# A RWKV-6 attention block with a SiLU MLP on one core: where a unit's first keys and another unit's diagonal are issued

## The chip, the cores and the metric

The kernel runs on one core of one Trainium2 chip. The metric is the device time of one execution in microseconds; the median of several executions is given. The core has five engines that take their instructions in order from queues of their own and wait for one another with semaphores: TensorE (PE in the profile, with its weight loads as PEld), VectorE (DVE), ScalarE (ACT), GpSimd (POOL) and SyncE (SP), which issues most of the DMAs here.

## The reference

Two blocks follow each other. The first is a linear attention with a decay per channel, over 4 batches, 8 heads, 768 tokens and a head size of 48:

```
for t in range(S):
    cur = einsum('bhd,bhe->bhde', u * k[t], v[t])
    y[t] = einsum('bhd,bhde->bhe', r[t], state + cur)
    state = w[t] * state + einsum('bhd,bhe->bhde', k[t], v[t])
```

The output y is laid out as 3072 tokens of 384 channels (all heads side by side) and is the input x of the second block, an MLP without gate:

```
h = x @ w_in            # 384 -> 2048
out = (h * sigmoid(h)) @ w_out   # 2048 -> 384
```

Everything is float32.

## The kernel before, in words

**Units.** The work is cut into 12 units. Unit i is one chunk of 128 tokens of two batches (all 8 heads); the units take the chunks in order, and the two pairs of batches in turn. Tokens or channels lie on the partitions as each step needs it. The first unit is number 0, so "the third unit" is `unit 2` in the code and below, and "the fourth" is `unit 3`.

**The attention of a unit.** Inside a chunk the score of a query against an earlier key needs the product of all decays between them. The kernel builds it in 7 levels. At level l the chunk is cut into blocks of 2^l tokens, and the queries in each odd block meet the keys in the even block ahead of it. Between the levels the keys and the queries are multiplied by the products of the decays of their blocks, so that after the last level they carry the decay to the ends of the chunk. The steps, with the names that stand in the code:

- `turn`: raw r, k and w are turned so that channels lie on the partitions (DVE's L374, from unit 2 on). The tiles are `tr`, `tk` and `tw`. `tk` has more rows than `tr`: in further places, called X, lie the keys that a level's scores read.
- `product` (POOL L422): products of neighbouring decays for the next level.
- `odd_ones` (ACT L659) copies keys of the odd blocks of level 0 into X, and `start_keys(own=True)` (POOL L669, two multiplies) writes the first multiplied keys there. Both together fill what level 1's scores read. `start_keys(own=False)` (two more of L669) multiplies keys in their own place, and is first needed by level 1's `odd_keys` (ACT L615).
- `grow_keys` (POOL L645, two multiplies) and `grow_queries` (DVE L627) go on to the next level. `prepare` makes the queries of a level in a new tile (DVE L779, ACT L781), so that two levels' scores can be computed in one `burst`.
- scores (PE L703 or L711) go to PSUM. Levels under 5 are copied into the tile `score` under a mask (DVE L721), levels 5 and 6 by plain copies of blocks (ACT L800, eight of 32 rows and four of 64).
- The diagonal: a token's own score is r*k*u summed over the channels, and since level 0 is computed along with it, a token's score against the one ahead of it too. `bonus` multiplies (POOL L448, L450, L452), `bonus_sum` sums (DVE L457, L461) and sends the sums by four small DMAs to their partitions (L467). `bonus_spread` copies them into the tile `both_b` (ACT: one L595 and four L597) and reverses the second batch's (DVE shuffle L598). `bonus_write` puts them into `score` under a mask (DVE L604, two copies of 128 x 1024 elements). Units 4 and later do the same for blocks of 8 tokens: `block_bonus` (POOL L507), `block_sum` (DVE L541) and `block_write` (DVE L577, of the same size as L604).
- `turn_apart`, `turn_k` (PE L819, ACT L827), `y_state`, `y_values` (PE L843, L850, L864) and `update` (PE L892) make y and the new state. L850 is the first that reads `score`.

**The MLP of a unit.** `up(i, m)`, m from 0 to 7, multiplies x with a slice of w_in (PE L1000, 12 instructions) into one of two PSUM buffers `p_h`, and ACT applies SiLU (L1009). From unit 1 on the second matrix is applied as a scheme of seven products of half size, `quarter(i, 0)` to `quarter(i, 6)` (PE L1066, 16 instructions each), that write into two PSUM buffers `p_o` in turn; `sums` (DVE L1048) makes the differences that the scheme multiplies, and DVE's L1075 (for quarter 0 ACT's L1073) takes each product out of PSUM. Unit 0's second matrix is applied plainly (`down`, PE L1022).

**Rounding of the weights.** The weights w_in and w_out come in 16 pieces of 768 KB. Each goes through ACT (L223, L225: `head_weight`; L231: `tail_weight`), DVE (L242, L243: `join_weight`) and POOL (L255: `add_weight`) before it is used. Pieces 10 to 15 run while unit 1's MLP and unit 2's attention begin; `piece(10 + m)` is followed by the list `others[m]`.

**What sets the order.** The order in which the Python code calls the steps is the order in every engine's queue; there is no scheduler that changes it. The calls for units 0 to 2 are written out by hand at L1107 to L1163. From unit 3 on `mix(i)` gives lists of steps for the attention of unit i, and between two lists the loop at L1165 puts one or two steps of the MLP of units i - 2 (`downs`: the quarters) and i - 1 (`ups`: up steps, with `sums`). For unit 3 the number of MLP steps behind each list is

```
room = (1, 1, 0, 2, 1, 1, 1, 1, 1, 2, 2, 1, 1) if i < NPAIR
```

so two up steps stand behind the list with `prepare(3, 5)`, and two behind the list with `burst(3, 5)`.

Of the kernel before, what the change touches and what calls it, by code (L numbers as in the profile page):

```python
# [38 lines left out]
def kernel(  # L39
# [11 lines left out]
    nc = tc.nc  # L51
# [4 lines left out]
    NL = 7  # L56
# [875 lines left out]
    def both(fn, i, *args):  # L932
        return [(fn, i, b, *args) for b in range(NB)]

    def block_loads(i, names="wkr"):
        return [(load_blocks, i, name, g) for name in names for g in range(4)]

    def mix(i):

        ahead = i + 1 < len(units)  # L940

        def at(now, *steps):
            return steps if now else ()

        def bonus_steps(j, *steps):
            return [(block_bonus, j, x) for x in steps]

        def sum_steps(j, *steps):
            return [(block_sum, j, x) for x in steps]

        def turns(j):
            return [*both(turn, j, "w"), (product, j, 0), *both(turn, j, "k")]

        def start(j):
            return [*[(product, j, l) for l in range(1, NL)], (grow_own, j, 1)]

        end = [[*at(ahead, *bonus_steps(i + 1, 0, 1, 2, 3))],
               [*at(i < len(units) - NB, (turn_apart, i), (turn_k, i)), (y_state, i), *both(y_values, i), *at(ahead, *turns(i + 1)),
                (sums, i - 1, FH // 2 - 2), *both(update, i), *at(not ahead, (move_x, i))]]
        if i < NPAIR:  # L960
            groups = [[*both(turn, i, "w"), (product, i, 0)],
                      [*both(turn, i, "k"), (odd_ones, i)], [*both(turn, i, "r"), (start_levels, i), (prepare_keys, i, 1)],
                      [(prepare, i, 1), *[(product, i, l) for l in range(1, NL)]],
                      [(burst, i, 1), (keep_level, i, 1)],
                      [(keep_level, i, 2), (go_on, i, 2)],
                      [(prepare, i, 3), (reverse_v, i), (bonus, i, 0)],
                      [(burst, i, 3), (keep_level, i, 3), (bonus_sum, i, 0), (bonus, i, 1), (bonus, i, 2)],
                      [(keep_level, i, 4), (go_on, i, 4), (bonus_sum, i, 1), (load_rk, i + 1), (load_u,)],
                      [(prepare, i, 5), (make_block_mask,), (bonus_spread, i), (bonus_write, i)],
                      [(burst, i, 5), (keep_level, i, 5), (keep_level, i, 6), (go_on, i, 6)], *end]  # L970
        else:
            groups = [[*both(turn, i, "r"), (grow_own, i, 0)], [*start(i), *sum_steps(i, 0, 1), *bonus_steps(i, 4, 5), (move_x, i - 1)],
                      [(odd_keys, i, 2), (grow_keys, i, 2, False), (grow_queries, i, 2), *sum_steps(i, 2)],
                      [(prepare, i, 3), *bonus_steps(i, 6, 7)],
                      [(burst, i, 3), (keep_level, i, 3), *sum_steps(i, 3, 4), (block_move, i), *at(ahead, (load_rk, i + 1))],
                      [(keep_level, i, 4), (go_on, i, 4)],
                      [(prepare, i, 5), (reverse_v, i)],
                      [(block_spread, i), (block_write, i)],
                      [(burst, i, 5), (keep_level, i, 5), (keep_level, i, 6), (go_on, i, 6)], *end]

        loads = [*at(i >= NPAIR and ahead, *block_loads(i + 1, "r")), *at(i + NSLOT < len(units), *block_loads(i + NSLOT, "wk"))]
        if i + 1 < len(units):
            loads.insert(len(loads) // 2, (load_values, i + 1))

        behind = groups[10 if i < NPAIR else 5 if i == NPAIR else 2:][:4 if i + NSLOT >= len(units) else None]
        for at, group in enumerate(behind):
            group += loads[at * len(loads) // len(behind):(at + 1) * len(loads) // len(behind)]
        return groups
# [114 lines left out]
    def back(fn, i, *args):  # L1103
# [8 lines left out]
    blocks = block_loads(2)  # L1112
    others = {1: [(clear, 0), (beat, 6)], 2: [(turn, 1, 0, "r"), (head_weight, 0), (beat, 2)],
              3: [(turn, 1, 1, "r"), (head_weight, 1), (beat, 2)], 4: [(turn, 1, 1, "w"), (reverse_v, 0)],
              5: [(bonus_spread, 0), (bonus_write, 0), (turn, 1, 0, "w")], 6: [*both(turn_in, 1, "k"), *blocks[0:4], (tail_weight, 0)]}
    for l in range(1, NL):
# [11 lines left out]
    others = {1: [(bonus_sum, 1, 0), (bonus_sum, 1, 1), (load_rk, 2), *blocks[8:12]], 2: [*both(update, 0)],  # L1128
              3: [(bonus_spread, 1), (reverse_v, 1), (clear, 1), (load_values, 2)]}
# [5 lines left out]
    for m in range(1, 4):  # L1135
# [6 lines left out]
       (join_weight, 9), (add_weight,), (tail_weight, 10), (head_weight, 10), *both(update, 1), (bonus_sum, 2, 1), (load_rk, 3), (up, 1, 0), *both(turn, 2, "w"))  # L1142
    blocks = block_loads(3)

    others = {0: [(up, 1, 1), (down, 0, 0, 0), *both(turn, 2, "k"), (product, 2, 0), (product, 2, 1)],
              1: [(up, 1, 2), *both(turn, 2, "r"), *[(product, 2, l) for l in range(2, NL)], *blocks[0:3]],
              2: [(down, 0, 0, 1), (odd_ones, 2), (start_keys, 2, nc.gpsimd, True), (grow_queries, 2, 0), *blocks[3:6]],
              3: [(up, 1, 3), (start_keys, 2, nc.gpsimd, False), (reverse_v, 2), *blocks[6:9]], 4: [(level, 2, 1), (up, 1, 4), *blocks[9:12]],
              5: [(down, 0, 0, 2), (up, 1, 5), (weight_sums, 0)]}
    for m in range(6):  # L1150
# [4 lines left out]
    blocks = block_loads(4)  # L1155
# [9 lines left out]
    for i in range(3, len(units)):  # L1165
        steps = downs(i - 2) + ups(i - 1)
        groups = mix(i)
        if i == NTOK + 1:
            groups[4].insert(1, (weight_sums, 3))
        room = (1, 1, 0, 2, 1, 1, 1, 1, 1, 2, 2, 1, 1) if i < NPAIR else (2, 1, 2, 2, 1, 1, 1, 2, 1, 1, 1)  # L1170
        for group, count in zip(groups, room):
            do(*group)
            for step in steps[:count]:
                do(*step)
            steps = steps[count:]
# [32 lines left out]
```

## Time and profile before

| | us |
|---|---|
| median of 3 runs | 598.59 (598.07 to 598.69) |
| the profiled execution | 599.11 |
| its span in the trace | 597.30 |
| PE busy | 587.5 |
| DVE busy | 411.6 |
| POOL busy | 351.5 |
| ACT busy | 232.7 |

The span is the time between the first and the last instruction of the trace; the other 1.81 us of the profiled execution lie around it. PE's busy time is nearly the whole span. Its granted clock was full throughout. In the timelines a row gives the start in us from the beginning of the span, the length in us, the engine, the line of the kernel, the operation, the tiles written and read, the size, how many instructions are put together in the row, and in brackets how long the engine was idle ahead of it and what it had waited for. In the list of waits a row names the waiting engine, tile and line, what it waited for, the total in us, how often, and the longest.

### The profile page before, as it was taken

The page shows a single profiled execution, that of the slowest core. Times are in us where ns is not written, and L with a number is a line of the kernel's source. Part 1 is how long each engine was busy: PE and PEld are TensorE (multiplying, and loading weights), DVE is VectorE, ACT ScalarE, POOL GpSimd, SP SyncE. Part 2 cuts the span into 40 slices and gives each one's busy share as a digit, 9 for nine tenths or more (in the row PEclk, how much of TensorE's full clock was granted, in tenths as well). Part 3 has the DMA queues.
Part 4 walks back from the last instruction along what each step waited for, and adds up shares of the span by engine and source line. Part 5 has one row for each costly group of instructions (what it writes and reads, how often), then busy time and mean ns, then how long its engine had stood idle before and what let it go on. Part 6 is the DMA issues. An engine that isn't in the chain of part 4 may idle for free.

```text
span 597.3 us, 14760 instructions
## 1 busy us (share of the span) xinstructions
PE 587.5 (98%) x5790; PEld 527.8 (88%) x5790; DVE 411.6 (69%) x709; ACT 232.7 (39%) x516; POOL 351.5 (59%) x414
## 2 busy tenths in 40 slices
PE   8999999999999999999999999999999999999997
PEld 7787866699899899899899899889889889889997
DVE  7879788798596695596696696686587587542041
ACT  6788874531530540440350351361351251250110
POOL 5998768447578568278378477477477567500000
PEclk9999999999999999999999999999999999999999
DMA  9965794443542543543543643643543531101000
GB/s 227 301 148 149 157 283 75 59 76 51 126 61 66 106 66 52 129 69 53 130 67 55 138 62 52 130 65 52 120 75 52 113 63 27 36 1 28 28 0 27
DMA packets 203078, 53.42 MB, mean 89 GB/s; under 512 B 186752, under 2 KB 194816, under 8 KB 203008
## 3 DMA queue, kind: packets, MB, share of 16 engines
q1 hardware_dynamic: 201424, 51.88, 42.7%
q8 instruction: 46, 0.75, 0.6%
q10 hardware_dynamic: 1584, 0.59, 0.5%
q14 instruction: 24, 0.20, 0.1%
HBM read 43.21 MB, written 5.24 MB: 81 GB/s over the span
## 4 chain that ended last, share of the span: by engine, by line
PE 82%; DVE 5%; POOL 4%; ACT 2%; SPq 2%; DMA 2%; issue 2%; POOLq 0%; DVEq 0%; ACTq 0%
PE p_h L1000 35%; PE p_o L1066 34%; PE p_m L1022 3%; PE p_m L864 2%; PE p_sc L703 2%; PE p_m L843 2%; SPq L123 2%; PE p_m L703 1%; DVE score L721 1%; POOL w_out_sb L255 1%; PE p_sc L892 1%; PE p_sc L819 1%; DMA own<-in_moe_w_out_dram 1%; DMA raw<-in_r_dram 1%; DVE score L604 1%
## 5 line engine op out<-in xcount | busy, mean ns | idle before, releaser
L1000 PE MATMUL p_h<-xt,w_in_sb 128*128 128x256 f32 x1152 | 259.8, 383 | 1.6 <-POOL tk L669 0.7
L1000 PEld LDWEIGHTS p_h<-xt,w_in_sb 128*128 128x128 f32 x1152 | 215.5, 190 | 33.3 <-ACT gt L1009 1.3
L1009 ACT ACTIVATE gt<-p_h 128x512 f32<-128x512 f32 x90 | 53.5, 595 | 172.5 <-PE p_h L1000 172.2
L645 POOL TENSOR_TENSOR tk<-tk,tw 128x256 f32<-128x256 f32 x128 | 93.9, 755 | 35.4 <-issue 21.0
L507 POOL TENSOR_TENSOR ruk<-tokens_rk 128x768 f32<-128x768 f32 (+1 forms) x32 | 51.4, 1616 | 64.4 <-DMA tokens_rk<-in_k_dram 34.6
L1066 PE MATMUL p_o<-own,temps 128*128 128x192 f32 x528 | 87.9, 326 | 0.0
L1066 PE MATMUL p_o<-w_out_sb,gt 128*128 128x192 f32 x508 | 86.4, 326 | 0.0
L1066 PEld LDWEIGHTS p_o<-own,temps 128*128 128x128 f32 x528 | 86.1, 190 | 0.1
L1066 PEld LDWEIGHTS p_o<-w_out_sb,gt 128*128 128x128 f32 x508 | 83.4, 190 | 0.6
L1048 DVE TENSOR_TENSOR temps<-gt 128x256 f32<-128x256 f32 x84 | 50.3, 599 | 25.7 <-ACT gt L1009 25.3
L627 DVE TENSOR_TENSOR tr<-tr,tw 128x512 f32<-128x512 f32 x61 | 54.1, 887 | 14.7 <-PE p_m L703 11.2
L422 POOL TENSOR_TENSOR tw<-tw 128x256 f32<-128x256 f32 (+6 forms) x83 | 40.4, 487 | 35.4 <-DVE tw L374 31.5
L615 ACT COPY tk<-tk 128x256 f32<-128x256 f32 x52 | 21.0, 403 | 102.6 <-POOL tk L645 80.1
L721 DVE COPY_PREDICATED score<-mask,p_sc 128x512 f32<-128x512 int8 x42 | 31.1, 796 | 3.2 <-PE p_sc L703 3.0
L1075 DVE TENSOR_TENSOR partial<-p_o,partial 128x192 f32<-128x192 f32 x33 | 11.7, 355 | 27.8 <-PE p_o L1066 27.8
L1066 PE MATMUL p_o<-w_out_sb,temps 128*128 128x192 f32 x176 | 30.4, 326 | 0.0
L1048 DVE TENSOR_TENSOR temps<-temps,gt 128x256 f32<-128x256 f32 x43 | 29.1, 677 | 1.5
L1075 DVE TENSOR_TENSOR temps<-p_o,partial 128x192 f32<-128x192 f32 x22 | 7.9, 358 | 31.5 <-PE p_o L1066 25.3
L541 DVE TENSOR_REDUCE block_sums<-ruk 128x4 f32<-128x192 f32 (+1 forms) x48 | 24.2, 545 | 7.1 <-POOL ruk L507 7.1
L1066 PEld LDWEIGHTS p_o<-w_out_sb,temps 128*128 128x128 f32 x176 | 28.9, 190 | 0.0
L869 ACT COPY yt<-p_m 48x512 f32<-48x512 f32 x40 | 23.2, 581 | 13.9 <-PE p_m L864 13.1
L703 PEld LDWEIGHTS p_sc<-tr,tk 48*64 48x64 f32 x960 | 17.3, 134 | 12.1 <-issue 7.7
(188 smaller groups left out, 814.2 us busy)
## 6 DMA issues: line engine op xcount, KB each, us to landing
w_out_sb<-in_moe_w_in_dram SPq DMA_DIRECT2D x6, 768.0 KB, 7.6
w_out_sb<-in_moe_w_out_dram SPq DMA_DIRECT2D x4, 768.0 KB, 6.4
own<-in_moe_w_out_dram SPq DMA_DIRECT2D x4, 768.0 KB, 6.1
tokens_rk<-in_r_dram SPq DMA_DIRECT2D x8, 384.0 KB, 4.5
tokens_rk<-in_k_dram SPq DMA_DIRECT2D x8, 384.0 KB, 5.4
tokens_w<-in_w_dram SPq DMA_DIRECT2D x8, 384.0 KB, 6.4
xt<-yt SPq DMA_DIRECT2D x60, 48.0 KB, 1.9
raw<-in_w_dram SPq DMA_DIRECT2D x80, 32.0 KB, 2.2
```

The source lines that it names most:

```text
L422: engine.tensor_tensor(out=up, in0=t[:, :, 0::2], in1=t[:, :, 1::2], op=ALU.mult)
L507: mul = lambda out, one, two: nc.gpsimd.tensor_tensor(out=out, in0=one, in1=two, op=ALU.mult)
L541: add = lambda out, have: nc.vector.tensor_reduce(out=out, in_=have, axis=mybir.AxisListType.X, op=ALU.add)
L627: nc.vector.tensor_tensor(out=odd, in0=odd, in1=tw[i][l][:, :, 0::2][:, :, :, None].to_broadcast([128, Q, L >> (l + 1), c]), op=ALU.mult)
L645: nc.gpsimd.tensor_tensor(out=out, in0=have, in1=odd_products(i, l, b, *blocks), op=ALU.mult)
L703: nc.tensor.matmul(to, lhsT=tk[i][rows, X[l % 2] + p, x * 64:(x + 1) * 64], rhs=have, start=True, stop=True)
L721: nc.vector.copy_predicated(out=dst, mask=masks[l][:, :, None].to_broadcast([128, NB, NP, ni, c]), data=sc[e].rearrange("p (b q) (i c) -> ...
L869: nc.scalar.copy(out=yt[i][PD * e:PD * e + D, x::2, :, :], in_=p_yt[i, e][PD * x:PD * x + D].rearrange("p (q b) t -> p q b t", b=NB))
L1000: nc.tensor.matmul(p_h[:, a, :], lhsT=w_in_sb[:, c, f * 128:(f + 1) * 128], rhs=xt[i][:, c, :], start=(c == 0), stop=(c == KC - 1))
L1009: nc.scalar.activation(out=gt[i, m], in_=p_h, func=AF.Silu)
L1048: nc.vector.tensor_tensor(out=out, in0=one, in1=two, op=op)
L1066: nc.tensor.matmul(p, lhsT=left(f), rhs=right[:, f, :], start=(f == 0), stop=(f == FH - 1))
```

## The change

Two groups of steps are called at another place.

In unit 2, `odd_ones` is called right behind the two turns of k, ahead of the first two products, and `start_keys(2, nc.gpsimd, True)` right behind the two turns of r, ahead of the other five products. Before, both were called one list later, behind piece 12 and a part of unit 0's `down`. `grow_queries(2, 0)` stays where it was.

In unit 3 (the only unit that comes by this branch of `mix`), `bonus_spread` and `bonus_write` are called behind `keep_level` of levels 5 and 6 and `go_on(3, 6)`. Before, they were called ahead of the two up steps that precede the burst.

```diff
-                      [(prepare, i, 5), (make_block_mask,), (bonus_spread, i), (bonus_write, i)],
-                      [(burst, i, 5), (keep_level, i, 5), (keep_level, i, 6), (go_on, i, 6)], *end]
+                      [(prepare, i, 5), (make_block_mask,)],
+                      [(burst, i, 5), (keep_level, i, 5), (keep_level, i, 6), (go_on, i, 6), (bonus_spread, i), (bonus_write, i)], *end]
...
-    others = {0: [(up, 1, 1), (down, 0, 0, 0), *both(turn, 2, "k"), (product, 2, 0), (product, 2, 1)],
-              1: [(up, 1, 2), *both(turn, 2, "r"), *[(product, 2, l) for l in range(2, NL)], *blocks[0:3]],
-              2: [(down, 0, 0, 1), (odd_ones, 2), (start_keys, 2, nc.gpsimd, True), (grow_queries, 2, 0), *blocks[3:6]],
+    others = {0: [(up, 1, 1), (down, 0, 0, 0), *both(turn, 2, "k"), (odd_ones, 2), (product, 2, 0), (product, 2, 1)],
+              1: [(up, 1, 2), *both(turn, 2, "r"), (start_keys, 2, nc.gpsimd, True), *[(product, 2, l) for l in range(2, NL)], *blocks[0:3]],
+              2: [(down, 0, 0, 1), (grow_queries, 2, 0), *blocks[3:6]],
```

The orders in PE's queue and in SP's queue are the same before and after. What moves on the others: one L659 on ACT and two L669 on POOL (unit 2); one L595 and four L597 on ACT, and one L598 and two L604 on DVE (unit 3). On DVE the L627 of `go_on(3, 6)` now stands ahead of them, and on ACT the twelve L800.

## The prediction

> **What bounds the kernel now.** I read the page's first part first, then the list of waits of TensorE alone, then the timelines of single engines around the two places that the change touches.
>
> ```profile
> PE 587.5 (98%) x5790; PEld 527.8 (88%) x5790; DVE 411.6 (69%) x709; ACT 232.7 (39%) x516; POOL 351.5 (59%) x414
> PEclk9999999999999999999999999999999999999999
> ```
>
> PE is busy for 98% of the span at full clock, and the change leaves its order as it is. So only a wait of PE that goes or comes can move the end. PE's own waits:
>
> ```profile
> PE p_sc L703 <- POOL tk L669: 1.5, 1, 1.5
> PE p_h L1000 <- ACT gt L1009: 0.6, 1, 0.6
> ```
>
> These two are what the change aims at. The first lies here:
>
> ```profile
> 88.57 1.30 POOL L669 TENSOR_TENSOR tk<-tk,tw 128x128 f32<-128x128 f32 x2
> 94.40 1.83 POOL L255 TENSOR_TENSOR w_out_sb<-temps 128x768 uint32<-128x768 uint32 x1 [1.51 <-ACT temps L223]
> 96.19 1.89 POOL L645 TENSOR_TENSOR tk<-tk,tw 128x256 f32<-128x256 f32 x2
> ...
> 89.92 0.70 PE L703 MATMUL p_sc<-tr,tk 48*64 48x64 f32 x32 [1.48 <-POOL tk L669]
> 98.51 0.69 PE L703 MATMUL p_sc<-tr,tk 48*64 48x64 f32 x32
> ```
>
> Level 1's scores of unit 2 wait 1.48 us for the first pair of L669. To be seen as well: level 2's scores (98.51) come only 0.43 us after the L645 pair they need (96.19 + 1.89 = 98.08). The second wait:
>
> ```profile
> 156.64 0.84 ACT L597 COPY both_b<-diag 32x16 f32<-32x16 f32 x4 [1.03 <-DMA diag<-own_sums]
> 157.39 1.06 ACT L1009 ACTIVATE gt<-p_h 128x512 f32<-128x512 f32 x2
> ...
> 158.03 8.39 PE L1000 MATMUL p_h<-xt,w_in_sb 128*128 128x256 f32 x36 [0.63 <-ACT gt L1009]
> ```
>
> ScalarE sits behind the small DMAs of the diagonal; two SiLUs queue behind it, and PE wants their PSUM bank.
>
> **Part one: first keys and ones of unit 2.** Moved: one ACT copy (L659) and one pair on POOL (L669). No DMA moves, and SP's order is the same. The copy takes 0.66 us and lands where ACT idles 1.34 us before 81.55 for a weight's DMA, so it costs nothing. On POOL the pair goes behind the L255 that ends at 83.73, so it is done at 83.73 + 1.30 = 85.0; PE, free of the previous matmuls at 85.69 + 2.75 = 88.4, waits no more. The five products behind it (1.66 us from 83.69) and the next L255 (86.46) slip by at most 1.3 and 0.2 us; the products that slip are first read after 100, and L255's block is read by PE at 93.2. If that cover went, it would be those 0.2 us.
>
> Gain at this place 1.5 us, but not to keep. The L645 pair at 96.19 is queued behind the L255 at 94.40, whose data come down a chain that starts with a weight's DMA landing at 89.5 (ACT then idle 1.56 us for it), which nothing here moves earlier. So the pair still ends at 98.08, and level 2's scores start at about 98.12 instead of 98.51. **Kept: 0.4 us**, with a new wait of PE of 1.1 us at 97.0. Ends: 0 (if the next tight place, the second scores of unit 3's first burst, started at 136.2 for POOL keys that are done at 135.54, gave it all back) and 0.4; I take 0.4, because POOL's chain before that place starts from PE's own matmuls and moves with them.
>
> **Part two: unit 3's diagonal.** Moved: five ACT copies (0.20 + 0.84 us), on DVE the shuffle (0.17) and two masked copies L604 (2.49 together), behind the twelve ACT copies of levels 5 and 6 and DVE's L627. On PE two things go: the 0.63 us, and a smaller one at 163.55, where the SiLU at 162.91 ended late. The single instructions there start 0.46 and 0.32 us apart instead of 0.22: 0.35 us. **Gain here 1.0 us**, 1.4 with part one, if nothing else becomes late.
>
> What becomes late is DVE. Times below have part one's 0.4 us taken off. ACT ends its SiLU at 156.5, copies levels 5 and 6 (2.25 + 1.50) until 160.3, and the diagonal (1.04) until 161.3; DVE shuffles, and L604 is ready at 161.6. The diagonal's DMAs have landed by then (156.6), so its waits on ACT are met. Behind it on ACT stands the SiLU of unit 2's fifth up step, done at 162.0; PE wants that bank at 162.3, so this is covered by 0.3 us. Before, it ran at 157.73, in 2.75 us of idle DVE time with POOL idle too. Now it falls on this:
>
> ```profile
> 161.67 1.80 POOL L507 TENSOR_TENSOR ruk<-tokens_rk 128x768 f32<-128x768 f32 x1 [6.28 <-DMA tokens_rk<-in_k_dram]
> 163.55 2.08 POOL L507 TENSOR_TENSOR ruk<-ruk,u_bc 128x768 f32<-128x768 f32 x1
> 165.59 1.18 POOL L507 TENSOR_TENSOR spare<-tokens_rk 128x384 f32<-128x384 f32 x1
> 166.85 1.08 POOL L507 TENSOR_TENSOR tokens_rk<-tokens_rk,tokens_w 128x384 f32<-128x384 f32 x1
> ...
> 163.54 0.42 DVE L1048 TENSOR_TENSOR temps<-gt 128x256 f32<-128x256 f32 x1 [2.75 <-ACT gt L1009]
> 164.00 1.92 DVE L1048 TENSOR_TENSOR temps<-temps,gt 128x256 f32<-128x256 f32 x1
> ```
>
> DVE and POOL take turns here: an L1048 of 0.42 us takes 1.92 while L507 runs, and the next ones 1.22 and 1.23. Is a masked copy held as well? No row shows it waiting. The nearest, unit 4's copy of the same shape, shows that it shuts POOL out:
>
> ```profile
> 204.25 2.51 POOL L507 TENSOR_TENSOR ruk<-tokens_rk 128x768 f32<-128x768 f32 x1 [4.04 <-DMA tokens_rk<-in_k_dram]
> ...
> 202.63 2.50 DVE L577 COPY_PREDICATED score<-spare 128x1024 f32<-128x1024 int8 x2
> 206.91 2.29 DVE L627 TENSOR_TENSOR tr<-tr,tw 128x512 f32<-128x512 f32 x1 [1.79 <-PE p_m L703]
> ```
>
> L507 takes 2.51 instead of 1.80 because it began inside the copy, and the L627 behind it (0.69 alone) 2.29. I take it that the two exclude each other in both orders. From 161.6 the two engines then do in turns: two copies of 1.25, four L507 (1.8, 1.67, 0.95, 0.92) and eight L1048, of which three run between POOL's at 0.3 and five at 0.37 (the rows above, less what each waited for the other). That is 2.5 + 5.3 + 2.7 = 10.5 us, until 172.1; before, the last L1048 ended at 169.68. **DVE is late by 2.4 us.** The lower end, if the copy runs beside POOL: L604 until 164.1, then the second L507, and the same turns: late by 0.2 to 0.7.
>
> [...] No run here yet shows a masked copy blocked by POOL.
>
> Who waits for DVE? L850 read the scores at 167.88 and now comes at 166.5; they are there between 165.8 and 167.3, a wait of up to 0.8 us that the later one below swallows. Behind the L1048s DVE has no idle time up to here:
>
> ```profile
> 179.90 0.36 DVE L1075 TENSOR_TENSOR temps<-p_o,partial 128x192 f32<-128x192 f32 x1
> ...
> 178.33 7.96 PE L1066 MATMUL p_o<-own,temps 128*128 128x192 f32 x48
> ```
>
> That L1075 frees the PSUM buffer of quarter 1 (p_o has two), which quarter 3 takes over. The 48 matmuls are quarters 2, 3 and 4 at 16 x 0.1625 = 2.6 us, so quarter 3 starts at 180.93, 0.67 us after the L1075 ends (180.26). This is the tight place. With DVE late by 2.4 the buffer is free at 182.66 and quarter 3 starts at 182.7: 1.8 us later than before, where PE would have come 1.4 earlier. Quarter 5 needs quarter 3's L1075 (185.30 + 0.35), late by the same 2.4: free at 188.05, PE there at 187.9, another 0.2 with the refill. Next, the burst at 191.4 needs POOL's L645s done by 189.56; late by 2.4 they end at 191.96, before PE's 193.9. Behind it every unit has microseconds of slack (in the next one DVE waits 0.55 us for quarter 1 instead of being late).
>
> **Sum**: 1.4 us of gain up to 178, all lost at quarter 3 and 5: 186.13 becomes 188.1, **+2.0 us**. Against the profiled execution (599.11 us; span 597.30 and 1.81 around it) that is 601.1; it lies 0.52 above the median of the runs, so the median becomes 598.59 + 2.0 = **600.6 us**.
>
> **Rivals.**
> - The copies run beside POOL: DVE late by 0.2 to 0.7, quarter 3 starts between 0.4 us earlier and 0.1 later, 598.2 to 598.7. For it: the same copy out of PSUM took 1.31 us beside POOL's multiply at 26.3. Against: that one has its data in PSUM, this one in SBUF, as L577. It decides below 0.67 us.
> - Faster: both waits go and quarter 3 isn't held, 1.4 us, 597.2. It needs L1075 done by 179.5, that is DVE 0.7 us earlier than before although 2.5 us of copies were put into its path; or a quarter that takes another buffer. Against it is the unbroken DVE row.
> - Worse: part one's 0.4 us is given back, so L604 is ready at 162.0, and POOL goes first each time: DVE late by 2.8 to 3.4, +2.4 to +3.0, 601.0 to 601.6.
> - The change doesn't do what it says in part one, its wait moving to 97 whole: contained above, 0.4 us.
>
> **How the numbers follow.** The forecast gets 0.60 (its own range 599.9 to 601.2, DVE late by 1.9 to 3.0), the copies beside POOL 0.20, faster 0.12, worse 0.08. The range leaves out the faster case and the upper part of the worst: 597.9 to 601.5. A measurement of this kernel tells about 0.2%, 1.2 us, from no change: slower by that has the forecast nearly whole and the worse case, 0.66; the rest of the forecast and the second case are 0.22; faster 0.12.
>
> **What would show it.** Right: no wait at 89.9, one of about 1.1 us for POOL's L645 near 97; L604 at 161.6 or later with at least one copy well over 1.3 us, or an L507 over 2.3; the last L1048 of unit 3 near 172; a wait of PE's L1066 for DVE's L1075 of 2 to 3 us near 180. Wrong: two copies of 1.3 us beside an undisturbed L507, or quarter 3 without a wait.

## The result: 0.31% slower, as forecast

| | us |
|---|---|
| before, median of 16 runs | 598.74 (597.06 to 601.19) |
| after, median of 16 runs | 600.50 (599.28 to 604.17) |
| ratio after to before | 1.0031, 95% interval 1.0018 to 1.0045 |
| profiled execution after | 601.43, span 599.6 (before 597.3) |

600.6 us had been forecast. (The two medians by themselves stand 1.76 us, or 0.29%, apart.) The same two kernels were timed once more on another chip: 601.31 against 598.96, ratio 1.0025 (1.0003 to 1.0047).

### The profile after

The page's first part and the list of PE's waits:

```profile
PE 589.0 (98%) x5790; PEld 529.4 (88%) x5790; DVE 415.2 (69%) x709; ACT 232.8 (39%) x516; POOL 351.7 (59%) x414
PEclk9999999999998999999999999999999999999999
```

```profile
PE p_o L1066 <- DVE temps L1075: 2.6, 1, 2.6
```

The waits for POOL's L669 and for ACT's gt are gone, and one of 2.6 us for DVE's L1075 is there in their place. PEclk has one slice with an 8; more of that below. Unit 2, on the timelines of POOL and of PE:

```profile
90.62 1.30 POOL L669 TENSOR_TENSOR tk<-tk,tw 128x128 f32<-128x128 f32 x2
93.01 1.82 POOL L255 TENSOR_TENSOR w_out_sb<-temps 128x768 uint32<-128x768 uint32 x1 [1.09 <-ACT temps L223]
94.80 1.88 POOL L645 TENSOR_TENSOR tk<-tk,tw 128x256 f32<-128x256 f32 x2
```

```profile
88.45 0.70 PE L703 MATMUL p_sc<-tr,tk 48*64 48x64 f32 x32
...
97.04 0.69 PE L703 MATMUL p_sc<-tr,tk 48*64 48x64 f32 x32
```

Neither group of scores waits. The L645 pair ends at 96.68, 1.4 us earlier than in the profile before: ACT's L223 at the head of the chain, which waits for a weight's DMA, ran at 88.09 instead of 89.51. Unit 3, on DVE and POOL:

```profile
160.47 4.12 DVE L604 COPY_PREDICATED score<-own_mask,both_b 128x1024 f32<-128x1024 int8 x2
164.49 2.03 DVE L1048 TENSOR_TENSOR temps<-gt 128x256 f32<-128x256 f32 x1
...
180.85 0.36 DVE L1075 TENSOR_TENSOR temps<-p_o,partial 128x192 f32<-128x192 f32 x1
```

```profile
161.18 2.24 POOL L507 TENSOR_TENSOR ruk<-tokens_rk 128x768 f32<-128x768 f32 x1 [7.24 <-DMA tokens_rk<-in_k_dram]
163.49 2.74 POOL L507 TENSOR_TENSOR ruk<-ruk,u_bc 128x768 f32<-128x768 f32 x1
```

The two copies took 2.49 us before and take 4.12 now; the two L507 took 1.80 and 2.08 and take 2.24 and 2.74. Where they overlap, DVE and POOL hold each other up. The L1075 that frees the PSUM buffer of quarter 1 comes at 180.85 instead of 179.90. On PE the 48 matmuls in one row before are now two rows, with quarter 5 behind them:

```profile
175.81 2.87 PE L1066 MATMUL p_o<-own,temps 128*128 128x192 f32 x16
181.26 7.15 PE L1066 MATMUL p_o<-own,temps 128*128 128x192 f32 x32 [2.58 <-DVE temps L1075]
188.24 2.76 PE L1066 MATMUL p_o<-w_out_sb,gt 128*128 128x192 f32 x16
```

Quarter 2 starts 2.52 us earlier than before (178.33), quarter 3 only 0.33 later (180.93), but quarter 5 comes 2.11 later (186.13). The row of 32 matmuls shows why: 7.15 us, where 32 x 0.1625 is 5.2. From 181.99 to 184.87 the single matmuls start 0.32 us apart instead of 0.16. Mean clock and busy time in three stretches (the columns are the stretch, its length, then busy time and instructions of PE, PEld, DVE, ACT and POOL, then PEclk, DMA share and GB/s):

```profile
178.00:181.20 3.20, 0.68 (x4) 0.39 (x3) 3.13 (x7) 0.41 (x1) 2.11 (x5) 1.00 0.41 51
181.20:185.20 4.00, 3.94 (x14) 3.94 (x15) 3.11 (x7) 0.00 (x0) 2.45 (x3) 0.57 0.25 57
185.20:196.00 10.80, 10.80 (x122) 10.38 (x121) 5.37 (x13) 0.92 (x2) 9.91 (x12) 1.00 0.17 56
```

The granted clock was 0.57 behind the wait. This was no step of the prediction. So the total agreed in this execution, and two of its terms did not: the last L1048 ended 0.95 us later than before instead of 2.4, and a stretch at half clock cost about 1.6. The experiments had to say which of the two is typical.

### The profile page after: what moved, and what is told of

It is laid out like the page before. It is cut to its first block, busy times and chain, and to the rows that moved or that the text cites. A ratio compares the mean times of both kernels' runs of the same rounds, so it can differ in the third digit from the quotient of the medians.

```text
span 599.6 us, 14759 instructions
## 1 busy us (share of the span) xinstructions
PE 589.0 (98%) x5790; PEld 529.4 (88%) x5790; DVE 415.2 (69%) x709; ACT 232.8 (39%) x516; POOL 351.7 (59%) x414
## 3 DMA queue, kind: packets, MB, share of 16 engines
HBM read 43.21 MB, written 5.24 MB: 81 GB/s over the span
## 4 chain that ended last, share of the span: by engine, by line
PE 87%; DVE 4%; POOL 3%; issue 1%; ACT 1%; DMA 1%; SPq 1%; POOLq 0%; DVEq 0%; ACTq 0%
PE p_h L1000 40%; PE p_o L1066 32%; PE p_m L1022 4%; PE p_m L864 2%; PE p_sc L703 2%; PE p_m L843 2%; PE p_m L703 1%; POOL w_in_sb L255 1%; POOL tk L645 1%; PE p_sc L892 1%; PE p_sc L819 1%; DMA raw<-in_r_dram 1%; DVE score L721 1%; DVE p_w L242 1%; DVE tr L627 1%
## 5 line engine op out<-in xcount | busy, mean ns | idle before, releaser
L645 POOL TENSOR_TENSOR tk<-tk,tw 128x256 f32<-128x256 f32 x128 | 93.7, 753 | 36.5 <-issue 22.0
L1066 PE MATMUL p_o<-own,temps 128*128 128x192 f32 x528 | 89.9, 331 | 2.6 <-DVE temps L1075 2.6
L1066 PEld LDWEIGHTS p_o<-own,temps 128*128 128x128 f32 x528 | 87.7, 193 | 3.1 <-DVE temps L1075 2.9
L507 POOL TENSOR_TENSOR ruk<-tokens_rk 128x768 f32<-128x768 f32 (+1 forms) x32 | 51.1, 1607 | 66.7 <-DMA tokens_rk<-in_k_dram 45.6
L1048 DVE TENSOR_TENSOR temps<-gt 128x256 f32<-128x256 f32 x84 | 53.8, 640 | 22.9 <-ACT gt L1009 22.6
L627 DVE TENSOR_TENSOR tr<-tr,tw 128x512 f32<-128x512 f32 x61 | 54.5, 893 | 16.9 <-PE p_m L703 13.4
L1075 DVE TENSOR_TENSOR partial<-p_o,partial 128x192 f32<-128x192 f32 x33 | 11.7, 355 | 28.4 <-PE p_o L1066 28.4
L1048 DVE TENSOR_TENSOR temps<-temps,gt 128x256 f32<-128x256 f32 x43 | 28.3, 659 | 1.5
L1075 DVE TENSOR_TENSOR temps<-p_o,partial 128x192 f32<-128x192 f32 x22 | 7.9, 358 | 30.4 <-PE p_o L1066 24.2
L654 POOL TENSOR_TENSOR tk<-tk,tw 128x256 f32<-128x256 f32 x32 | 27.6, 883 | 0.0
```

The source lines that it names most:

```text
L507: mul = lambda out, one, two: nc.gpsimd.tensor_tensor(out=out, in0=one, in1=two, op=ALU.mult)
L627: nc.vector.tensor_tensor(out=odd, in0=odd, in1=tw[i][l][:, :, 0::2][:, :, :, None].to_broadcast([128, Q, L >> (l + 1), c]), op=ALU.mult)
L645: nc.gpsimd.tensor_tensor(out=out, in0=have, in1=odd_products(i, l, b, *blocks), op=ALU.mult)
L654: nc.gpsimd.tensor_tensor(out=have, in0=have, in1=odd_products(i, l, b, [2, NP * ni]), op=ALU.mult)
L1048: nc.vector.tensor_tensor(out=out, in0=one, in1=two, op=op)
L1066: nc.tensor.matmul(p, lhsT=left(f), rhs=right[:, f, :], start=(f == 0), stop=(f == FH - 1))
```

## Experiments

The theory: the diagonal's copies and POOL's L507 exclude each other, so DVE frees the PSUM buffer late and PE waits for it. The main rivals: the loss is the half clock; or DVE's sum of work.

### The kernel before, once more

No edit.

> The kernel before once more, for a second profile. If the landing of unit 2's weight DMAs differs from one execution to the next, ScalarE's L223 near 89.5 starts a microsecond or more earlier or later here, though nothing is changed. If it was the moved steps that brought these landings forward, L223 starts at 89.5 again (within 0.2 us). The wait for the first pair (1.5 us) and the wait behind the diagonal (0.6 us) are there in both cases.

Measured: 599.0 us, span 597.2 (before's median there 598.21). PE's waits in unit 2 and for the diagonal:

```profile
PE p_h L1000 <- ACT gt L1009: 1.0, 1, 1.0
...
PE p_sc L703 <- POOL tk L669: 0.4, 1, 0.4
```

With nothing altered the wait that part one removes was 0.4 instead of 1.5 us: PE came to these scores 0.8 us later (at 89.22 instead of 88.44), and the L669 pair ended 0.3 us earlier (at 89.59 instead of 89.87). The gt wait was 1.0 instead of 0.6, and L223 ran at 88.69 instead of 89.51. Quarter 5 started at 186.16 (186.13 before), so these differences cancel. A wait in one profile is a sample.

### One part at a time

```diff
 e1_keys_only: only the lines of others = {...} as in the change
 e2_diag_only: only the lines of mix(i) as in the change
```

> Unit 2's part alone; the diagonal stays where it was. My account: the wait at 89.9 goes, 0.4 to 1.5 us of it are kept up to 158 by when the weight's DMA lands; the masked copies meet no L507; quarter 3 waits at most 0.8 us for the L1075 and no half clock follows: faster by 0.4 to 1.2 us, 597.5 to 598.3. Rival, unit 2's part does the harm (POOL's new order makes something late): slower than before, up to the 1.9 us of the whole change.

> Unit 3's part alone. My account: PE comes 1.0 us earlier to the quarters of unit 2, the masked copies and L507 hold each other up, the last L1048 of unit 3 ends 2 to 2.8 us later, quarter 3 waits 2.4 to 3 us and starts 1.5 to 2.2 us later than before; if the wait costs clock as it did in the whole change, another 1.5 us: slower by 2 to 3.7 us, 600.6 to 602.3. Rival, the copies run beside POOL: within 0.5 us of before. Rival, unit 2's part does the harm: faster by 1.0 us.

| | median, us | ratio to before |
|---|---|---|
| keys only | 598.77 (596.81 to 601.11) | 1.0004 (0.9988 to 1.0020) |
| diagonal only | 600.12 (599.22 to 601.30) | 1.0027 (1.0016 to 1.0037) |

The loss lies in part two. Part one takes its wait away (none for L669 in that profile, quarter 5 at 184.67), but its gain is not to be seen in the medians: the expected 0.4 to 1.2 us was not measured. In the profile of the diagonal alone, on DVE and PE:

```profile
160.84 5.01 DVE L604 COPY_PREDICATED score<-own_mask,both_b 128x1024 f32<-128x1024 int8 x2
```

```profile
180.88 5.47 PE L1066 MATMUL p_o<-own,temps 128*128 128x192 f32 x32 [1.78 <-DVE temps L1075]
...
241.50 4.77 PE L1000 MATMUL p_h<-xt,w_in_sb 128*128 128x256 f32 x21 [1.83 <-DMA xt<-yt]
```

The masked copies are slower still, L1075 is waited for, and the 32 matmuls stand at full clock (5.47 us). The expectation held in kind and missed in its sizes: the wait was 1.78 us instead of 2.4 to 3, quarter 3 started where it did before (180.88), and the median is 1.9 us above before's instead of 2 to 3.7. In this execution an early start hides the loss. PE came to the burst of levels 5 and 6 at 155.13, 1.1 us earlier than in the first profile of before (156.24), since it had waited only 0.3 us for L669. From there to quarter 5 (186.27) it took 31.1 us, against 29.9 and 30.2 in the two profiles of before. A DMA of move_x that landed after 3.5 us instead of 2.0 at most cost another 1.83 us at 241.5; that wait is taken up below. None of the twelve executions had a mean clock of 0.998 or less, and they were slower all the same, so the loss does not need the half clock.

### The diagonal out of PSUM

e3: the change, with one more ACT copy that puts unit 3's diagonal into free columns of a PSUM bank, so that L604 reads its data there and not in SBUF:

```diff
-        diag[i] = both_b
+        diag[i] = both_b if i < NPAIR - 1 else banks["p_sc"][0][:, 512 - NB * H * 2:].rearrange("p (b h s) -> p b h s", b=NB, h=H)
+        _ = i < NPAIR - 1 or nc.scalar.copy(out=diag[i], in_=both_b)
```

> The whole change, but unit 3's diagonal is copied once more by ScalarE into 32 free columns of a PSUM bank, and the masked copies read it there: the same copies at nearly the same place in every queue, with one SBUF input instead of two. My account: the two copies take 1.3 us each although L507 runs, L507 stays at 1.8, the last L1048 ends within 0.5 us of before (169.7), quarter 3 waits 1 to 2 us, which is too short for the half clock (the wait of 1.5 us at 89.9 in the kernel before cost none): faster than before by 0.2 to 1.2 us, 597.4 to 598.4. Rival, what counts is only that the copies stand later in DVE's queue: slower than before by about the 1.9 us of the whole change.

Measured: 598.26 us (597.59 to 601.57), ratio to before 0.9999 (0.9985 to 1.0014). DVE, POOL and PE:

```profile
160.77 2.50 DVE L604 COPY_PREDICATED score<-own_mask,p_sc 128x1024 f32<-128x1024 int8 x2 [0.26 <-ACT p_sc L600]
```

```profile
160.05 1.81 POOL L507 TENSOR_TENSOR ruk<-tokens_rk 128x768 f32<-128x768 f32 x1 [6.04 <-DMA tokens_rk<-in_k_dram]
162.14 1.81 POOL L507 TENSOR_TENSOR ruk<-ruk,u_bc 128x768 f32<-128x768 f32 x1 [0.28 <-DMA u_bc<-in_u_dram]
```

```profile
176.18 8.27 PE L1066 MATMUL p_o<-own,temps 128*128 128x192 f32 x48
```

This is the decisive run. At the same place, beside the same L507, both engines run at their undisturbed length once one operand of the copy comes from PSUM: 2.50 us for the pair of copies (2.49 in the kernel before), 1.81 for each L507 (1.80 for the first there). DVE's last L1048 of this group ends at 168.34 instead of 170.63, the 48 matmuls are one row again, and the harm is gone. The 0.2 to 1.2 us by which this kernel had been expected to beat the one before are not to be seen, though: its median there is 598.21. DVE's number of instructions and their sum of undisturbed work are those of the change, so the second rival falls: the loss is what the copies and L507 cost each other where both operands of the copy lie in SBUF.

### Keeping PE busy through the wait

e4: the change with eight matmuls of ident by ident, whose results are not used, ahead of quarter 3:

```diff
+        for x in range(8 * ((i, which) == (NTOK, 3))): nc.tensor.matmul(banks["p_m"][0][:, 0:128], lhsT=ident, rhs=ident, start=True, stop=True)
```

> The changed kernel with eight 128x128 matmuls of ident by ident (no use is made of them, into a bank of p_m that is free) ahead of the down step's quarter 3 of the third unit, which in the changed kernel starts at 181.26 after 2.58 us of idle PE and then runs ten of its matmuls 0.32 us apart instead of 0.16. Theory (the idle stretch itself halves the clock, and the wait is set by DVE): the eight matmuls end before 180.9, quarter 3 starts at 181.2 to 181.5 all the same, its matmuls stand 0.16 apart, quarter 5 starts 1.3 to 1.8 us earlier than 188.24 and the kernel is 1.0 to 1.8 us faster than the changed one, so 0.2 to 1.4 us slower than before. Rival (the slow matmuls come from something else that falls on this place, weight loads or the reading of temps): ten matmuls of quarter 3 stay 0.32 apart and the time stays at 600.5, within 0.4.

Measured: 600.46 us (599.01 to 604.10), ratio to before 1.0020 (0.9999 to 1.0041); span 598.2. Quarter 3 started at 181.60, no matmul was at half spacing, quarter 5 started at 186.98, 1.26 us earlier than in the change's first profile. But the median did not move, against the expectation. The next run says why.

### The change, twice more

No edit (e7 and e8); the second of them was timed as well.

> The changed kernel once more, with nothing altered, for what differs from one execution to the next. Theory: L604 again above 4.0 us beside L507, the first L1075 near 180.8, PE's wait for it 1.8 to 3.0 us; if the half clock of quarter 3 follows from this wait, ten matmuls or so again stand 0.32 apart when the wait is above 2.3 us, and none when it is below 1.9. Rival for the clock (an accident of one execution): a wait above 2.3 us with all matmuls 0.16 apart. The weights' transfer that the ACT L223 at 88 to 90 waits for lands anywhere in 88.0 to 89.6.

> The changed kernel, nothing altered, for its time beside the next three. Theory: 1.2 to 2.4 us slower than before; in the profile a wait of PE for L1075 of 1.8 to 3.0 us; half clock behind it only where the mean granted clock of the execution is 0.997 or below, which about one execution in five shows, so it is no part of the median. Rival: half clock behind the wait in this execution too, with a mean clock of 0.998 or below in most of the timed executions.

Measured: 600.97 us, span 599.1; and a median of 601.31 us (600.32 to 603.23), with a profiled execution of 603.22, span 601.4. PE of the first:

```profile
98.10 0.70 PE L703 MATMUL p_sc<-tr,tk 48*64 48x64 f32 x32 [0.86 <-POOL tk L645]
```

```profile
177.06 2.87 PE L1066 MATMUL p_o<-own,temps 128*128 128x192 f32 x16
182.50 5.47 PE L1066 MATMUL p_o<-own,temps 128*128 128x192 f32 x32 [2.58 <-DVE temps L1075]
187.89 2.87 PE L1066 MATMUL p_o<-w_out_sb,gt 128*128 128x192 f32 x16
```

The same wait of 2.58 us, and all matmuls at full clock: the half clock came behind one of two waits of 2.58 us (the last section sets the executions side by side) and is not a term of the change. Without the 5 of the change's 28 timed executions whose mean clock was 0.998 or less, its two medians are 600.25 and 601.3 us instead of 600.50 and 601.31. That fits the dummy matmuls, which gained nothing. In the second execution a later start stands in place of the half clock: L223 ran at 89.46, the L645 pair ended at 98.05, and PE waited for it at 98.10, so all that follows stands 1.25 us later than in the first profile. The three executions of the change and others, side by side (us):

| kernel | L223 | wait in unit 2 | wait for gt | L604, both | last L1048 ends | wait for L1075 | quarter 3 | quarter 5 | wait for xt |
|---|---|---|---|---|---|---|---|---|---|
| before | 89.51 | 1.5 | 0.6 | 2.49 | 169.68 | 0 | 180.93 | 186.13 | 0 |
| before again | 88.69 | 0.4 | 1.0 | 2.49 | 169.75 | 0 | - | 186.16 | 0 |
| change | 88.09 | 0 | 0 | 4.12 | 170.63 | 2.58 | 181.26 | 188.24 | 0 |
| change, 2nd | 89.46 | 0.9 | 0 | 4.12 | 171.87 | 2.58 | 182.50 | 187.89 | 0 |
| change, 3rd | 90.34 | 1.0 | 0 | 5.02 | 172.04 | 1.78 | 182.66 | 188.04 | 2.0 |
| diagonal only | 87.69 | 0.3 | 0 | 5.01 | 170.25 | 1.78 | 180.88 | 186.27 | 1.8 |
| diagonal in PSUM | 87.91 | 0 | 0 | 2.50 | 168.34 | 0 | - | 184.37 | 0.6 |

The wait in unit 2 is for L669 where part one is missing, and for L645 in the change. A dash: no row of its own starts there. Where L507 began ahead of the copies (5.0 us), less of POOL's four L507 is left beside the L1048s, and the wait for L1075 is 1.78 instead of 2.58 us. Quarter 5 comes at 187.9 to 188.2 in all three executions of the change.

### The copies out of PSUM first

DVE's L1075 of quarters 1 to 3 ahead of the turn of r and the block sums (DVE's order alone); first in the change (e5), then in the kernel before (e9):

```diff
+        if i == NPAIR:
+            one, two, three = groups[0:3]
+            cut = [n for n, (fn, *_) in enumerate(two) if fn is block_sum][0]
+            groups[0:3] = [[], one, two[:cut], two[cut:], three[:-1], three[-1:]]
+            room = (2, 0, 1, 0, 1, 1, *room[3:])
```

> The changed kernel with DVE's L1075 of the third unit's quarters 1, 2 and 3 put ahead of the turn of r, the products' block sums and the last of them (DVE's order alone changes). Theory (PE waits because L1075 stands on DVE behind two L374 of 0.7 us and an L627 of 1.0 us, and DVE is late by the slow L604): L604 stays at 4 to 5 us, but the first L1075 starts at 178.5 to 179.0 instead of 180.85, PE's wait for it is 0.2 to 0.8 us instead of 2.58, no matmul of quarter 3 runs at half spacing, quarter 5 starts 3 to 4 us earlier than 188.24, and the kernel is 2.0 to 4.0 us faster than the changed one: 596.5 to 598.5. Rival (the loss sits in DVE's sum of work, so that the turn of r, now later by 0.4 to 1 us, makes the next unit's matmuls wait instead): quarter 3 starts early, but a wait of PE for DVE or ACT of 1.5 us or more appears behind quarter 5, and the time is within 1 us of 600.5.

> The kernel before, with DVE's L1075 of the third unit's quarters 1 to 3 ahead of the turn of r and the block sums, and nothing else. Theory (in the kernel before DVE is ahead of PE at this place: L1075 starts at 179.9 while quarter 2 ends at 180.9): no wait is there to be taken away, so within 0.5 us of before. Rival (the order of the copies is itself what makes the kernel with both apart faster than before): 0.8 to 2 us faster than before.

Measured in the change: 600.39 us (598.34 to 604.21), ratio to before 1.0022 (0.9998 to 1.0045); in the kernel before: 598.73 us, ratio 0.9986 (0.9968 to 1.0004), no difference, as expected. PE in the change with the copies first:

```profile
177.73 8.06 PE L1066 MATMUL p_o<-own,temps 128*128 128x192 f32 x48
185.68 2.87 PE L1066 MATMUL p_o<-w_out_sb,gt 128*128 128x192 f32 x16
```

L604 was at its slowest (the two together took 5.59 us, until 167.2), L1075 started at 179.58, and PE did not wait: quarter 5 came 2.2 us before that of the change's second execution, and no wait for DVE or ACT of 1.5 us appeared behind it. So the place of L1075 in DVE's queue is where the lateness reaches PE. The time followed only in part. Of the 2.2 us the profiled execution kept 1.5 (599.48 against 600.97); a wait for xt took 0.5. In the median 2 to 4 us had been expected, and next to nothing is to be seen: the ratio to before is 1.0022 where the change alone had 1.0031 and 1.0025, which lies within the intervals. Four of the twelve executions had a mean clock of 0.994 to 0.997; the other eight have a median of 599.55, against 598.84 for before's on that chip counted in the same way. So the rival's time came without its mechanism, the path by way of L1075 is shown in the profile and not in the median, and what else the median lost stays open.

### Both apart, and without the earlier diagonal's new place

e6: the change and the copies first, with the diagonal between the two up steps ahead of level 5's burst, and one up step between level 5's and level 6's copies. e10: the keys' part of the change and the copies first, the diagonal as in the kernel before. e11 is e6 once more, beside e10. The edit of e6 in its main lines:

```diff
-                      [(prepare, i, 5), (make_block_mask,)],
-                      [(burst, i, 5), (keep_level, i, 5), (keep_level, i, 6), (go_on, i, 6), (bonus_spread, i), (bonus_write, i)], *end]
+                      [(prepare, i, 5), (make_block_mask,)], [(bonus_spread, i), (bonus_write, i)],
+                      [(burst, i, 5), (keep_level, i, 5)], [(keep_level, i, 6), (go_on, i, 6)], *end]
...
-        room = (1, 1, 0, 2, 1, 1, 1, 1, 1, 2, 2, 1, 1) if i < NPAIR else (2, 1, 2, 2, 1, 1, 1, 2, 1, 1, 1)
+        room = (1, 1, 0, 2, 1, 1, 1, 1, 1, 1, 1, 1, 1, 1, 1) if i < NPAIR else (2, 1, 2, 2, 1, 1, 1, 2, 1, 1, 1)
...
```

> The kernel of e5_copies_first with the third unit's diagonal (L595 to L604) between the two up steps ahead of level 5's burst instead of behind level 6's copies, and one up step between level 5's and level 6's copies. Theory (the slow L604 and the place of L1075 are the whole loss): L604 starts before L507 does, at 156 to 158, in 2.5 to 3.0 us, the last L1048 of the up steps ends before 169.0, quarter 3 starts at 178.5 to 179.2, no wait of PE for L1075 above 0.5 us; 595.8 to 597.8, which is 0.5 to 2.5 us faster than before. Rival (the copies for the up step's gt on ACT then come late, since level 6's copies follow an up step's L1009): a wait of PE for ACT's L800 or L1009 of 1 us or more near 155 to 162, and 598 to 600.

> The second unit's part of the change together with the copies first, the third unit's diagonal left as before. Theory (the keys' part takes 0.4 to 1.5 us off, the copies' order nothing, and the diagonal was best left ahead of the burst): 0.3 to 1.5 us faster than before, and not slower than the kernel with both apart by more than 0.5 us. Rival (the gain of the kernel with both apart comes from its up step between the copies of levels 5 and 6): no faster than before by more than 0.2 us, and 0.8 us or more slower than the kernel with both apart.

> The kernel of e6_both_apart once more, with nothing altered, beside the two above: it was 0.28% faster than before. Theory: 0.5 to 2 us faster than before again, and within 0.5 us of e10_keys_copies. Rival: 0.8 us or more faster than e10_keys_copies; or no faster than before, where the first measurement was an accident.

| | median, us | ratio to before |
|---|---|---|
| e6 | 597.84 (597.06 to 599.01) | 0.9972 (0.9956 to 0.9989) |
| e11, the same again | 598.14 (596.92 to 601.73) | 0.9980 (0.9959 to 1.0001) |
| e10 | 599.04 (597.86 to 603.38) | 0.9995 (0.9974 to 1.0017) |

Both apart is faster than the kernel before by 0.2 to 0.3%; its second interval just touches no change, and its first median lies just above the 595.8 to 597.8 that had been expected. The medians of e10 and e11 stand 0.9 us apart, as the rival of e10 said and not the theory: the gain comes from where the diagonal and the up steps stand. Their intervals overlap, so this is likely and not certain. ACT and PE in e10 show what is gained:

```profile
156.71 0.20 ACT L595 COPY both_b<-diag 128x16 f32<-128x16 f32 x1 [4.20 <-DMA diag<-own_sums]
157.94 0.84 ACT L597 COPY both_b<-diag 32x16 f32<-32x16 f32 x4 [1.03 <-DMA diag<-own_sums]
158.69 1.06 ACT L1009 ACTIVATE gt<-p_h 128x512 f32<-128x512 f32 x2
```

```profile
159.32 3.14 PE L1000 MATMUL p_h<-xt,w_in_sb 128*128 128x256 f32 x9 [2.75 <-ACT gt L1009]
```

In the order of the kernel before two SiLUs stand behind L595, which waits for the diagonal's small DMAs. L595 started at 153.96 in e1, 155.41 in the first profile, 155.46 in the second of before, 156.22 in e9 and 156.71 here, and PE's wait for gt went with it: 0, 0.6, 1.0, 1.8 and 2.7 us. The DMAs themselves took 1.7 to 1.8 us from issue to landing in all five; what moved is when SP issued them. SP in e1 and in e10 (SPq is its queue of DMA issues):

```profile
141.97 7.85 SPq L123 DMA_DIRECT2D raw<-in_r_dram  x16
...
151.40 2.47 SPq L467 DMA_DIRECT2D diag<-own_sums  x4
```

```profile
143.90 9.34 SPq L123 DMA_DIRECT2D raw<-in_r_dram  x16
...
154.31 2.44 SPq L467 DMA_DIRECT2D diag<-own_sums  x4
```

The 16 issues ahead of them began later in e10, and one of the 16 took 1.95 us instead of 0.45. In e6 and e11 one of the two SiLUs runs ahead of L595, and PE waits 0.9 (at 163.1, behind the copies of level 5) and 0 us for gt. The change removes this wait as well (none in any profile of it) and pays more for it on DVE.

## Why the prediction was right

**What bounds the kernel.** Right: PE's order is unchanged, and the loss shows as one new wait of PE, at the named place. What is paid there stays: in all fourteen profiles the span is 597.3 us, plus what quarter 5 started later than 186.13 (or less what it started earlier), plus the wait for xt, within 0.3 us.

**Part one, kept 0.4 us.** Its mechanism is right and its size was below what can be told. The wait for L669 goes in every profile with this part. The new one for L645 was 0.9 and 1.0 us where L223 ran at 89.46 and 90.34 (1.1 forecast for 89.5), and did not come at 88.09. The sentence that nothing moves L223's DMA is right for the change, but executions move it by 2.7 us (87.69 to 90.34), which the step took as fixed. The products behind the moved pair took 2.2 us instead of the 1.66 that the step counted on, so the next L255 came at 87.05 and 87.23, 0.6 to 0.8 us later instead of 0.2; nothing waited for it. The median of part one alone is +0.04%, its interval from -0.12 to +0.20%.

**Part two, gain 1.0 us.** Right in kind; the wait taken away is a spread of 0 to 2.7 us by when SP issues the diagonal's DMAs, of which the profile before held one value.

**"I take it that the two exclude each other in both orders."** Right, and this step decided the sign. It was the author's assumption: the profile before had a row for L507 held up by a masked copy (2.51 us instead of 1.80), and none for the other order. The runs showed both: with two SBUF inputs the pair of copies took 4.12 to 5.59 us beside L507, with one from PSUM 2.50; and a first L507 that began inside the copies took 2.24 to 2.49 us instead of 1.80.

**DVE late by 2.4 us.** The forecast times were L604 at 161.6, the last L1048 until 172.1, quarter 3 at 182.7, quarter 5 at 188.1. Second execution: 161.72, 171.87, 182.50, 187.89. Third: 162.60, 172.04, 182.66, 188.04. In the first they were 160.47, 170.63 and 181.26, since PE and ACT came 1.25 us earlier there, and the half clock then gave 188.24. From the start of L604 to the end of the last L1048 it was 10.2, 10.2 and 9.4 us, against a forecast of 10.5. So the second execution agrees by the forecast's own steps; in the third L604 started 1.0 us late and the turns were 1.1 us short, and in the first the half clock made up for an early start: these two agreements are luck. The mean of quarter 5 over the three, 188.06, less 186.15 before, is +1.9 us, against a forecast of +2.0; without the 1.6 us of half clock in the first it is +1.4.

**The sum.** +2.0 us forecast; +1.76 and +2.35 between medians. The rival with the copies beside POOL (598.2 to 598.7) did not come as such; with the diagonal in PSUM it did, at 598.26. Its cover is the one named there: data in PSUM. The 1.4 us of gain up to 178 are not confirmed by any median: neither part one alone nor the change with the diagonal in PSUM was faster than before.

**Not in the prediction**: the wait for xt at 241 to 243 us. It is there in the third execution of the change, with the diagonal alone and in e10, 1.4 to 2.0 us each, where a DMA of move_x landed after 3.3 to 3.7 us instead of 2.0; in the two profiles of before there was none. In e3, e5 and e11 PE came earlier and waited 0.4 to 0.7 us with landings of 2.0 us at most. Whether the change makes this wait likelier was not tried and stays open.

## What to carry to other kernels

Before a step is moved into a gap of one engine, look at what the other engines do in that gap: two masked copies on VectorE that took 2.5 us became 4.1 to 5.6 beside GpSimd's multiplies, and one operand in PSUM set it right. Follow a late engine to its next instruction that frees a buffer, for that is where the lateness was paid here (1.78 to 2.58 us at L1075). And take a wait behind a DMA as a sample (the one for gt was 0.6 and 1.0 us in two profiles of the kernel before): a second profile of the same kernel shows what of it is the kernel's.

## What the hardware showed that was not expected

**Half clock behind short waits.** PE's matmuls ran at half spacing for 3.4 us after waits of 2.58 us (the change's first profile), 1.75 (e9) and 2.75 (e10). A stretch of e9, in the columns given above:

```profile
158.80:162.30 3.50, 3.47 (x9) 2.76 (x10) 2.79 (x3) 2.62 (x10) 0.00 (x0) 0.54 1.05 277
162.30:170.00 7.70, 7.70 (x77) 6.64 (x79) 5.59 (x7) 3.93 (x9) 5.84 (x4) 0.99 0.43 55
```

After waits of 2.58 (the second execution), 1.78 (twice) and 2.0 us no such stretch came. Each costs about 1.6 us, which is nine or ten of the quarters' matmuls at double spacing, and such an execution shows a mean clock of about 0.997. Of the timed executions 7 of 93 of the kernel before in the three later series had one of 0.998 or less, and 5 of 28 of the change.

All three stretches last 3.41 us, and the recorded stretches of full clock are whole numbers of steps of 3.413 us: in the change's first profile from 4.20 to 181.70, which is 52 such steps, and in the profile before from 5.24 to 599.16 and in the change's second from 4.11 to 598.03, which is 174 each. So in the second a step begins at 4.11 + 52 x 3.413 = 181.60. The two steps around the wait, in the first profile and in the second:

```profile
178.28:181.70 3.42, 0.84 (x6) 0.55 (x5) 3.35 (x6) 0.41 (x1) 1.87 (x4) 1.00 0.40 49
181.70:185.11 3.41, 3.41 (x12) 3.41 (x12) 2.60 (x5) 0.00 (x0) 2.36 (x2) 0.50 0.23 59
```

```profile
178.19:181.60 3.41, 1.74 (x11) 1.31 (x9) 3.34 (x7) 0.06 (x1) 2.99 (x7) 1.00 0.41 48
181.60:185.02 3.42, 2.52 (x15) 2.52 (x16) 3.39 (x7) 0.35 (x1) 1.03 (x2) 1.00 0.29 57
```

In the first the wait of 2.58 us lies whole in one step, which leaves PE 0.84 us of work, and the next step runs at half clock. In the second the same wait is split over two steps, with 1.74 and 2.52 us of work, and the clock stays. The steps ahead of the other two half clocks had 1.67 us of work (e9) and 1.12 (e10). A step with 1.63 us (the wait of 1.78 with the diagonal alone) cost no clock. So 0.84, 1.12 and 1.67 us of work in a step stood ahead of a half clock, and 1.63, 1.74 and 2.52 did not; what decides between 1.63 and 1.67 was not shown.

**Transfers and issues spread by microseconds with nothing changed.** The same weight's DMA let ACT's L223 start between 87.69 and 90.34 us. A single DMA issue of SP took 1.35 to 1.95 us instead of 0.45 in both profiles of before, in e9 and in e10, and none did in e1; with it the start of L595 went from 153.96 to 156.71. The two waits of PE that the change was aimed at came to 0.3 to 1.5 and to 0 to 2.7 us in the profiles that have them, a spread as large as the whole change is worth.
